# Sparse attention and an ELU feed-forward layer on one core: both halves of a pair's scores issued as one group

## The chip, the cores and the metric

The kernel runs on 1 core of one Trainium2 chip. The metric is the device time of one execution in microseconds, here the median of several runs.

## The reference

Attention over 8 batches, 8 heads, 576 positions, 64 features per head, and behind it a feed-forward layer on the 4608 tokens:

```python
scores = scale * np.matmul(q, k.transpose(0, 1, 3, 2))
mask_local = (rel >= 0) & (rel < stride)                     # heads 0 to 3, stride 32
mask_strided = (rel >= 0) & (pos[None, :] % stride == pos[:, None] % stride)   # heads 4 to 7
...
attn = np.exp(scores)
attn = attn / (np.sum(attn, axis=-1, keepdims=True) + 1e-09)
...
h = x @ w_in                                                 # 512 to 2048
g = np.where(h > 0.0, h, alpha * (np.exp(np.minimum(h, 0.0)) - 1.0))
return (g @ w_out).astype(np.float32)                        # 2048 to 512
```

## The kernel before

**The work.** Each batch has four "pairs" of heads (class `Pair`): s0 and s1 (strided heads), l0 and l1 (local heads). A pair's scores are computed in two halves, u = 0 and 1, as small blocks: a local half has 6 blocks of 128 keys by 96 queries, a strided one 4 blocks of 126 by 126 (u = 0) or 6 of 108 by 108 (u = 1). A score matmul contracts over the 64 features of one head, so it uses 64 rows of TensorE's array; the blocks alternate between the array's upper and lower 64 rows, and the two row halves write to two different PSUM banks (`bank` in `blocks`, L385). `scores(u)` (L413) is: the matmuls into the double bank `pair_a` (L422), one exp on ScalarE from both banks at once (L430), and the multiplication by the mask on VectorE (L437). `av(u)` (L442) multiplies the probabilities by v, whose extra column of ones gives the sum (L454, full array), into a bank of the ring; VectorE takes the reciprocal (L462) and writes the normalised x (L463). `x_out` (L478) transposes x into `xT`. For strided pairs it does five transposes on TensorE (L490) into a ring bank and two ScalarE copies (L497, L499); the first two transposes read what av(0) left, the other three what av(1) left. For local pairs of batches 0 to 3 there are six transposes (L503) and a copy (L507, on VectorE from batch 2 on), the fourth to the sixth for av(1); from batch 4 on a DMA transpose on SP's queue does it (L482).

`transposes` (`t_q`, `t_k`) brings q and k into the layout that scores need, on TensorE with a ring bank and a ScalarE copy. DMA transposes do it instead from batch 3 on for strided pairs (`BY_DMA = 3`) and from batch 4 on for local ones (`EARLY = 4`).

**The feed-forward layer.** Tokens go in nine chunks of 512. `moe_in(nb, m)` (L545) does four 128x512 matmuls into a bank of the ring `hps` (L534), exp on ScalarE (L556) and two VectorE operations that make ELU of it (L563, L565). `moe_out(nb, i)` (L569) does four matmuls into a bank of `ops` (L575); four such calls fill one output block, which ScalarE copies to o_sb (L579) and SP stores (L581).

**The order of the work.** It is written out by hand. Stage nb of the last loop interleaves, for s = 0 to 15, moe_in(nb, s) and moe_out(nb - 1, s), with the attention of batch nb + 1 in between: before each moe_in is an even gap (2s), before each moe_out an odd one (2s + 1). `attention(b, start, pitch, at)` puts pair i's pieces at gap start + pitch * i + offset, with the offsets `at` in the order t_q, t_k, scores(0), scores(1), av(0), av(1), x_out, v_in. From batch 3 on start is 2 and pitch 7, so the four pairs' scores(0) come at gaps 2, 9, 16 and 23. Batch 3 has its strided pairs first, batches 4 to 7 have the local ones first. Each engine works through its own instructions in this order. `halo` (a VectorE copy inside v_loc) stands at av(1)'s offset less 2, for batches before the fifth.

**PSUM.** There are eight banks of 512 floats a partition: `pair_a` (two), `half0` and `half1`, and `single0` to `single3`. `share` says which of them each use takes: `sc` (scores), `hps`, `ops`, `ring` (av, transposes, x_out). A `Ring` gives the bank that was handed out longest ago; whoever is to write it waits for the readers of its last content. Up to batch 3 (stages 1 and 2) hps is half0 and half1, and the ring is single0 to single2. From batch 4 on hps is half0, half1 and single0, and the ring single1 and single2. ops is single3.

The functions that the change touches, and what calls them:

Of the kernel before, what the change touches and what calls it, by code (L numbers as in the profile page):

```python
# [10 lines left out]
F32 = mybir.dt.float32  # L11
# [3 lines left out]
ACT = mybir.ActivationFunctionType  # L15
# [15 lines left out]


PIECES = (-2, -1, 0, 2, 3, 5, 7, 0)
TIMES = (
    None,
    (4, 6, (-3, -2, 0, 2, 4, 6, 9, 3)),
    (6, 6, (-3, -2, 0, 2, 4, 6, 8, 0)),
    (2, 7, PIECES),
)


# [15 lines left out]
def kernel(  # L57
# [9 lines left out]
    nc = tc.nc  # L67
# [4 lines left out]
    scale = 1.0 / float(D) ** 0.5  # L72
# [16 lines left out]
    pair_a = ps.tile([128, 2, 512], F32, tag="pair_a")  # L89
    singles = [ps.tile([128, 512], F32, tag=f"single{i}", name=f"single{i}")  # L90
               for i in range(4)]

    used = []

    class Ring:
# [3 lines left out]
        def next(self):  # L99

            for bank in self.banks:
                if all(bank is not u for u in used):
                    break
            else:
                bank = next(u for u in used if any(u is b for b in self.banks))
                used[:] = [u for u in used if u is not bank]
            used.append(bank)
            return bank


    rings = {}

    def share(sc, hps, ops, ring):
        rings.update(sc=Ring(*sc), hps=Ring(*hps), ops=Ring(*ops), ring=Ring(*ring))
# [41 lines left out]
    EARLY = 4  # L156

    BY_DMA = 3
# [46 lines left out]
    def transpose_batch(b):  # L205

        if b >= BY_DMA:
            for name, to in (("q", qT), ("k", kT)):
                nc.sync.dma_start_transpose(out=to["str"][b % 2],
                                            in_=nat[name, "str"][b % 3])  # L210
        if b >= EARLY:
            for name, to, o in (("q", qT, 0), ("k", kT, 32)):
                for a in range(2):
                    nc.sync.dma_start_transpose(
                        out=to["loc"][b % 2][:, a, o:o + 640].rearrange(
                            "p (i r) -> p i r", r=128),
                        in_=nat[name, "loc"][b % 3][:, 640 * a:640 * a + 640])

    def load_batch(b):
        for name in "qkv":  # L220
            load_strided(b, name)
        for name in "qkv":
            load_local(b, name)
# [97 lines left out]
    class Pair:  # L321
# [89 lines left out]
                nc.vector.tensor_copy(t[0:32, :, 1:6, 0:D], t[96:128, :, 0:5, 0:D])  # L411

        def scores(self, u):  # L413
            sc = rings["sc"].next()
            blocks = self.blocks(u)
            for p, blk, bank, i, nk, nq in blocks:
                at, half = self.place(p, blk)
                d = slice(64 * half, 64 * half + 64)
                kind = "str" if self.strided else "loc"
                c = 0 if self.strided else LB * blk  # L420

                nc.tensor.matmul(sc[:, bank, i * nq:(i + 1) * nq],  # L422
                                 lhsT=kT[kind][self.b % 2][d, at, c:c + 128],
                                 rhs=qT[kind][self.b % 2][d, at, c:c + nq],
                                 start=True, stop=True)
            nk, nq = blocks[0][4:]
            w = len(blocks) // 2 * nq
            pr = (p_p if self.b else p_p0).tile([128, 648], BF16, tag="pr", name="pr")
            halves = pr[0:nk, 0:2 * w].rearrange("k (a x) -> k a x", a=2)
            nc.scalar.activation(halves, sc[0:nk, :, 0:w], ACT.Exp, scale=scale)  # L430
            if not self.strided:
                m = mask_l[:, 288 * u:288 * (u + 1)]
            elif u == 0:
                m = mask_s[0:126, 0:252]
            else:
                m = mask_s3[0:108, 0:324]
            nc.vector.tensor_tensor(halves, halves,  # L437
                                    m.unsqueeze(1).to_broadcast([nk, 2, w]),
                                    op=ALU.mult)
            self.pr[u] = pr  # L440
# [68 lines left out]
    def attention(b, start, pitch, at):  # L509


        gaps = {}
        pairs = [Pair(b, s, hp) for s in (b < EARLY, b >= EARLY) for hp in range(2)]
        if b >= EARLY:
            gaps[start] = [pairs[3].halo]
        for i, pr in enumerate(pairs):
            for off, piece in ((at[0], pr.t_q), (at[1], pr.t_k),
                               (at[7], lambda pr=pr: pr.v_in(0)),
                               (at[7] + (b > 1), lambda pr=pr: pr.v_in(1)),
                               (at[2], lambda pr=pr: pr.scores(0)),  # L520
                               (at[3], lambda pr=pr: pr.scores(1)),
                               (at[4], lambda pr=pr: pr.av(0)),
                               (at[5], lambda pr=pr: pr.av(1)),
                               (at[6] + (b > 1 and pr.strided), pr.x_out), (at[5] - 2, pr.halo if b < EARLY else lambda: None)):
                gaps.setdefault(start + pitch * i + off, []).append(piece)
        return gaps

# [10 lines left out]
    def moe_ahead(c, start, stop):  # L538

        for m in range(AHEAD):  # L540
            if start:
                ahead[m] = rings["hps"].next()
            moe_chunk(0, m, c, ahead[m], start, stop)
# [25 lines left out]
    def moe_out(nb, i):  # L569
        kk, part = divmod(i, 4)  # L570
        if part == 0:
            state["ops"] = rings["ops"].next()
        ops = state["ops"]
        for m in range(4 * part, 4 * part + 4):
            nc.tensor.matmul(ops, lhsT=g_of[nb][:, m, kk * 128:(kk + 1) * 128],  # L575
                             rhs=w_out_sb[:, m, :], start=(m == 0), stop=(m == MC - 1))
        if part == 3:
            o_sb = p_o.tile([128, d_model], F32, tag="o_sb", name="o_sb")
            nc.scalar.copy(o_sb, ops)  # L579
            r0 = nb * N_TILE + kk * 128  # L580
            nc.sync.dma_start(out=out[r0:r0 + 128, :], in_=o_sb)  # L581
# [19 lines left out]
    def range_flag(row_ok16):  # L601
        cnt = rings["ring"].next()
        nc.tensor.matmul(cnt[0:1, 0:1], lhsT=row_ok16, rhs=ones, start=True, stop=True)
        nc.vector.tensor_scalar(flag, cnt[0:1, 0:1], scalar1=127.5, scalar2=None,
                                op0=ALU.is_le)

    def run(gaps, keys):
        for gap in sorted(g for g in gaps if g in keys):
            for piece in gaps[gap]:
                piece()  # L610

    every = range(-10, 1000)
    pairs = {p.name: p for p in (Pair(0, s, hp) for s in (True, False) for hp in range(2))}
    parts = [s for s in OPENING if s.startswith("moe")]
    for step in OPENING:
        pair, what = step.split(".")
        if pair == "moe":
            if step == parts[0]:

                ps_open.close()  # L620
                ps_h = inner.enter_context(tc.tile_pool(name="ps_h", bufs=1, space=PSUM))
                b_halves = [ps_h.tile([128, 512], F32, tag=f"half{i}", name=f"half{i}")
                            for i in range(2)]
                rings["hps"] = Ring(*b_halves, singles[3])
            moe_ahead(int(what), step == parts[0], step == parts[-1])
        else:
            pairs[pair].step(what)
# [13 lines left out]
    for nb in range(n_chunks + 1):  # L641

        if nb + 1 < B:
            gaps = attention(nb + 1, *TIMES[min(nb + 1, 3)])
            if nb == 0:
                share([pair_a], b_halves + singles[3:], [], singles[:3])
            elif nb + 1 < EARLY:
                share([pair_a], b_halves, singles[3:], singles[:3])
            else:
                share([pair_a], b_halves + singles[:1], singles[3:], singles[1:3])  # L650
        else:
            gaps = {}
            share([], b_halves + singles[:1], singles[2:], singles[1:2])
        if nb + 3 < B:
            load_batch(nb + 3)
        for s in range(MC):
            if s == 6 and nb > 0 and nb + 2 < B:
                transpose_batch(nb + 2)
            run(gaps, (2 * s,) if s else range(-10, 1))
            if nb < n_chunks:  # L660
                moe_in(nb, s)
            run(gaps, (2 * s + 1,))
            if nb == B and s == 4:
                range_flag(row_ok16)
            if nb > 0:
                moe_out(nb - 1, s)
        run(gaps, range(2 * MC, 1000))
        if nb + 1 == B:
            row_ok16 = range_check()
# [163 lines left out]
```

## Time and profile before

| what | value |
|---|---|
| median of 3 runs | 335.62 us (335.5 to 335.96) |
| the profiled execution | 335.16 us |
| its span, first to last instruction | 333.4 us |
| TensorE matmuls | 309.0 us busy, 93% of the span |
| VectorE | 246.6 us, 74% |
| ScalarE | 177.0 us, 53% |
| chain that ended last, share of TensorE | 86% |
| mean granted TensorE clock | 0.988 |

PE is TensorE's matmuls, PEld its weight loads, DVE is VectorE, ACT is ScalarE, POOL is GpSimd, SP is the queue of output stores and DMA transposes. In a timeline each row has the start in us from the span's start, the duration, engine, line, operation, what is written and read, the shapes, and how many such instructions were merged into the row (x4). Matmuls are pipelined: the end of one is modelled and lies behind the start of the next, so on TensorE distances of starts are to be read. Some matmul records are missing from the trace (x3 where four were issued). Idle time before an instruction stands in brackets with who ended it.

### The profile page before, as it was taken

How to read it: one execution, taken by the hardware profiler on the slowest of the kernel's cores; microseconds unless marked ns; L12 is line 12 of the kernel's file. 1: busy time of each engine (PE TensorE's matmuls, PEld its weight loads, DVE VectorE, ACT ScalarE, POOL GpSimd, SP SyncE). 2: the span in 40 equal slices, each digit the busy share in tenths (PEclk: the TensorE clock that was granted, in tenths of full speed). 3: DMA queues.
4: the chain of work that ended last, by engine and by line, in shares of the span. 5: the costliest groups of instructions: out<-in, count | busy, mean ns of one | idle time of the engine just before them, and what ended most of it. 6: DMA issues, size and time to landing. Idle time of an engine off the chain costs nothing.

```text
span 333.4 us, 6112 instructions
## 1 busy us (share of the span) xinstructions
PE 309.0 (93%) x2198; PEld 151.8 (46%) x2238; DVE 246.6 (74%) x536; ACT 177.0 (53%) x316; POOL 146.6 (44%) x233
## 2 busy tenths in 40 slices
PE   1887888999999999999999999999999999999993
PEld 0563554455544454444444444444444444444441
DVE  6684699797778778898788878887887666766500
ACT  3744788676555664555655554556555434444220
POOL 8976774998389679919943850000000000000000
PEclk9999699999999999999999999999999999999999
DMA  6999999999989999999998995900110010000111
GB/s 103 144 132 164 161 205 128 122 136 145 161 118 136 148 177 110 112 136 170 169 142 120 166 93 114 142 33 34 49 49 33 31 66 31 31 34 33 64 64 70
DMA packets 102523, 35.68 MB, mean 107 GB/s; under 512 B 80269, under 2 KB 97877, under 8 KB 102485
## 3 DMA queue, kind: packets, MB, share of 16 engines
q0 software_dynamic: 68016, 18.10, 56.6%
q1 hardware_dynamic: 34469, 17.11, 25.7%
q8 instruction: 19, 0.31, 0.4%
q14 instruction: 19, 0.16, 0.2%
HBM read 36.70 MB, written 9.44 MB: 138 GB/s over the span
## 4 chain that ended last, share of the span: by engine, by line
PE 86%; ACT 4%; DVE 4%; issue 2%; DMA 2%; SPq 1%; DVEq 0%; ACTq 0%
PE single L575 37%; PE half L534 28%; PE single L534 9%; PE pair_a L422 4%; PE single L454 4%; DMA q_stage<-in_q_dram 2%; PE single L366 1%; ACT pr L430 1%; PE single L490 1%; SPq L173 1%; PE single L352 1%; ACT e_sb L556 1%; PE single L503 1%; DVE x_l L463 1%; DVE g_sb L565 1%
## 5 line engine op out<-in xcount | busy, mean ns | idle before, releaser
L575 PE MATMUL single<-w_out_sb,g_sb 128*128 128x512 bf16 x561 | 143.4, 379 | 1.1 <-issue 0.5
L534 PE MATMUL half<-xT,w_in_sb 128*128 128x512 bf16 x410 | 110.9, 387 | 2.1 <-issue 1.0
L556 ACT ACTIVATE e_sb<-half 128x512 f32<-128x512 f32 x107 | 63.9, 597 | 79.3 <-PE half L534 74.0
L563 DVE TENSOR_SCALAR e_sb<-e_sb 128x512 bf16<-128x512 f32 x139 | 62.3, 448 | 48.5 <-ACT e_sb L556 46.0
L575 PEld LDWEIGHTS <-g_sb 128*128 128x128 bf16 x576 | 52.9, 98 | 58.9 <-issue 1.1
L534 PEld LDWEIGHTS <-w_in_sb 128*128 128x128 bf16 x576 | 51.9, 100 | 55.4 <-issue 3.7
L565 DVE TENSOR_TENSOR g_sb<-e_sb,half 128x512 bf16<-128x512 bf16 x102 | 70.2, 688 | 3.8
L430 ACT ACTIVATE pr<-pair_a 128x576 bf16<-128x576 f32 (+2 forms) x60 | 39.0, 650 | 12.1 <-PE pair_a L422 11.9
L534 PE MATMUL single<-xT,w_in_sb 128*128 128x512 bf16 x141 | 38.6, 386 | 0.6 <-issue 0.2
L556 ACT ACTIVATE e_sb<-single 128x512 f32<-128x512 f32 x37 | 22.1, 598 | 26.6 <-PE single L534 23.5
L579 ACT COPY o_sb<-single 128x512 f32<-128x512 f32 x36 | 21.1, 587 | 19.1 <-PE single L575 18.4
L173 POOL DMA_DIRECT2D v_raw<-in_v_dram x32 | 20.8, 701 | 19.8 <-DVE v_str L405 17.8
L454 PEld LDWEIGHTS <-pr 128*128 128x128 bf16 (+3 forms) x352 | 21.8, 111 | 16.1 <-issue 3.3
L565 DVE TENSOR_TENSOR g_sb<-e_sb,single 128x512 bf16<-128x512 bf16 x37 | 25.5, 688 | 1.4
L185 POOL DMA_DIRECT2D v_loc<-in_v_dram x32 | 24.5, 816 | 1.4 <-PE pair_a L422 0.7
L173 POOL DMA_DIRECT2D k_str<-in_k_dram x32 | 20.0, 644 | 5.3 <-DMA w_out_sb<-in_moe_w_out_dram 2.9
L173 POOL DMA_DIRECT2D q_str<-in_q_dram x28 | 17.3, 631 | 7.5 <-DMA k_loc<-in_k_dram 4.5
L463 DVE TENSOR_TENSOR x_l<-single,rden 96x384 bf16<-96x384 f32 x32 | 17.7, 554 | 1.1
L463 DVE TENSOR_TENSOR x_s<-single,rden 126x256 bf16<-126x256 f32 (+1 forms) x32 | 15.7, 491 | 1.1
L437 DVE TENSOR_TENSOR pr<-pr,mask_l 128x576 bf16<-128x576 bf16 x32 | 14.4, 453 | 2.3 <-ACT pr L430 2.0
L437 DVE TENSOR_TENSOR pr<-pr,mask_s 126x504 bf16<-126x504 bf16 (+1 forms) x32 | 14.5, 455 | 1.2 <-ACT pr L430 1.2
L197 POOL DMA_DIRECT2D k_loc<-in_k_dram x16 | 12.4, 786 | 1.8 <-PE half L534 0.8
(96 smaller groups left out, 244.6 us busy)
## 6 DMA issues: line engine op xcount, KB each, us to landing
out_dram<-o_sb SPq DMA_DIRECT2D x36, 256.0 KB, 2.5
v_loc<-in_v_dram POOLq DMA_DIRECT2D x32, 72.0 KB, 5.0
k_str<-in_k_dram POOLq DMA_DIRECT2D x32, 67.5 KB, 4.1
v_raw<-in_v_dram POOLq DMA_DIRECT2D x32, 67.5 KB, 4.4
w_in_sb<-in_moe_w_in_dram POOLq DMA_DIRECT2D x4, 512.0 KB, 8.1
w_out_sb<-in_moe_w_out_dram POOLq DMA_DIRECT2D x4, 512.0 KB, 12.6
q_str<-in_q_dram POOLq DMA_DIRECT2D x28, 67.5 KB, 5.5
q_loc<-in_q_dram POOLq DMA_DIRECT2D x4, 288.0 KB, 6.9
```

The lines of the kernel that those rows point to most:

```text
L173: engine.dma_start(out=t[0:108, h].rearrange("p g d -> p (g d)"), in_=rows[h, :, 0:30, :].rearrange("t (r g) d -> t r (g d)", g=5))
L185: nc.gpsimd.dma_start(out=v_loc[b % 3][32:128, h, :, :D], in_=v[b, h].rearrange("(i p) d -> p i d", p=LB))
L430: nc.scalar.activation(halves, sc[0:nk, :, 0:w], ACT.Exp, scale=scale)
L437: nc.vector.tensor_tensor(halves, halves, m.unsqueeze(1).to_broadcast([nk, 2, w]), op=ALU.mult)
L454: nc.tensor.matmul(av[0:m, p, blk - b0, :], lhsT=self.pr[u][0:nk, o:o + m], rhs=vt[0:nk, 2 * self.hp + p, blk, :], start=True, stop=True)
L463: nc.vector.tensor_tensor(self.x[0:nq, b0:b0 + n].rearrange("q g p d -> q p g d"), av[0:nq, :, 0:n, 0:D], r.unsqueeze(3).to_broadcast([nq, ...
L534: nc.tensor.matmul(hps, lhsT=w_in_sb[:, c, m * 128:(m + 1) * 128], rhs=xT[:, c, nb * N_TILE:(nb + 1) * N_TILE], start=start, stop=stop)
L556: nc.scalar.activation(e_sb, hps, ACT.Exp)
L563: nc.vector.tensor_scalar(e1_sb, e_sb, scalar1=1.0, scalar2=1.0, op0=ALU.min, op1=ALU.subtract)
L565: nc.vector.tensor_tensor(g_of[nb][:, m, :], e1_sb, hps, op=ALU.max)
L575: nc.tensor.matmul(ops, lhsT=g_of[nb][:, m, kk * 128:(kk + 1) * 128], rhs=w_out_sb[:, m, :], start=(m == 0), stop=(m == MC - 1))
L579: nc.scalar.copy(o_sb, ops)
```

## The change

From batch 3 on (`b >= BY_DMA`) scores(1) no longer goes to `pair_a`, but to half0 and half1, one row half of the array into each, and stands in the same gap as scores(0), right behind it. Its exp becomes two activations, one for each bank. So the matmuls of both halves follow one another, 12 for a local pair and 10 for a strided one.

The offsets change with it: scores(0) and scores(1) at 0 (before: 0 and 2), av(0) at 3 (as before), av(1) at 4 (5), x_out at 6 (7 for local pairs and 8 for strided ones; the extra gap of strided pairs stays for batch 2 alone). halo, tied to av(1), comes a gap earlier in batch 3.

The banks change places: half0 and half1 become the ring (in stage 2 with single0, later alone), and hps takes single1 and single2 (stage 2) or single0 to single2 (later). How many banks each use has stays as it was. scores(1) takes both halves whenever it runs, and they count as handed out last.

```diff
+WHOLE = (-2, -1, 0, 0, 3, 4, 6, 0)
 TIMES = (
...
-    (2, 7, PIECES),
+    (2, 7, WHOLE),
 )
...
         def scores(self, u):
-            sc = rings["sc"].next()
+            if self.b >= BY_DMA and u == 1:
+                halves = b_halves
+                used[:] = [x for x in used if all(x is not h for h in halves)] + halves
+                sc = [halves[0][:, None, :], halves[1][:, None, :]]
+                sc = [(h, slice(i, i + 1)) for i, h in enumerate(sc)]
+            else:
+                sc = [(rings["sc"].next(), slice(0, 2))]
...
-                nc.tensor.matmul(sc[:, bank, i * nq:(i + 1) * nq],
+                tile_, of = next((t, a) for t, a in sc if a.start <= bank < a.stop)
+                nc.tensor.matmul(tile_[:, bank - of.start, i * nq:(i + 1) * nq],
...
-            nc.scalar.activation(halves, sc[0:nk, :, 0:w], ACT.Exp, scale=scale)
+            for t, of in sc:
+                nc.scalar.activation(halves[:, of], t[0:nk, :, 0:w], ACT.Exp, scale=scale)
...
-                               (at[6] + (b > 1 and pr.strided), pr.x_out), (at[5] - 2, pr.halo if b < EARLY else lambda: None)):
+                               (at[6] + (b == 2 and pr.strided), pr.x_out), (at[5] - 2, pr.halo if b < EARLY else lambda: None)):
...
-            elif nb + 1 < EARLY:
+            elif nb + 1 < BY_DMA:
                 share([pair_a], b_halves, singles[3:], singles[:3])
+            elif nb + 1 < EARLY:
+                share([pair_a], singles[1:3], singles[3:], b_halves + singles[:1])
             else:
-                share([pair_a], b_halves + singles[:1], singles[3:], singles[1:3])
+                share([pair_a], singles[:3], singles[3:], b_halves)
         else:
             gaps = {}
-            share([], b_halves + singles[:1], singles[2:], singles[1:2])
+            share([], singles[:3], singles[3:] + b_halves[:1], b_halves[1:])
```

## The prediction

> **What bounds the kernel now.** I read the page first, then the timeline of TensorE, then those of VectorE and ScalarE, in a stage that does the matmuls of one token chunk and the attention of a batch from the fourth on. The page's first part:
>
> ```profile
> PE 309.0 (93%) x2198; PEld 151.8 (46%) x2238; DVE 246.6 (74%) x536; ACT 177.0 (53%) x316; POOL 146.6 (44%) x233
> ```
>
> The waits put only 0.5 us of TensorE's idle time between 93 and 300 us to another engine. So there its instruction stream is the time, and what it saves or newly waits for is won or lost whole. Its timeline (start, duration, line):
>
> ```profile
> 179.26 0.32 PE L422 MATMUL pair_a<-qT_str,kT_str 64*128 64x108 bf16 x6
> 179.51 1.04 PE L534 MATMUL half<-xT,w_in_sb 128*128 128x512 bf16 x4
> 180.38 0.32 PE L454 MATMUL single<-v_str,pr 126*128 126x65 bf16 x4
> 180.54 1.03 PE L575 MATMUL single<-w_out_sb,g_sb 128*128 128x512 bf16 x4
> 181.40 1.03 PE L534 MATMUL half<-xT,w_in_sb 128*128 128x512 bf16 x4
> 182.26 0.37 PE L454 MATMUL single<-v_str,pr 108*128 108x65 bf16 x6
> 182.47 1.03 PE L575 MATMUL single<-w_out_sb,g_sb 128*128 128x512 bf16 x4
> 183.34 1.03 PE L534 MATMUL single<-xT,w_in_sb 128*128 128x512 bf16 x4
> 184.30 0.28 PE L422 MATMUL pair_a<-qT_str,kT_str 64*128 64x126 bf16 x4
> ```
>
> Read the distances of starts, not the durations, which overlap. Four big matmuls last 0.86 us until the next group (180.54 to 181.40), but 0.96 when a score group follows (183.34 to 184.30), and 0.87 right after one (179.51 to 180.38). So a score group costs 0.10 us to enter and 0.01 behind it. Then VectorE and ScalarE:
>
> ```profile
> 182.31 0.17 DVE L462 RECIPROCAL rden<-single 126x4 f32<-126x4 f32 x1
> 182.52 0.42 DVE L463 TENSOR_TENSOR x_s<-single,rden 126x256 bf16<-126x256 f32 x1
> 183.10 0.43 DVE L563 TENSOR_SCALAR e_sb<-e_sb 128x512 bf16<-128x512 f32 x1 [0.15 <-ACT e_sb L556]
> 183.56 0.69 DVE L565 TENSOR_TENSOR g_sb<-e_sb,half 128x512 bf16<-128x512 bf16 x1
> 184.16 0.19 DVE L462 RECIPROCAL rden<-single 108x6 f32<-108x6 f32 x1
> 184.39 0.56 DVE L463 TENSOR_TENSOR x_s<-single,rden 108x384 bf16<-108x384 f32 x1
> ```
>
> ```profile
> 184.40 0.60 ACT L556 ACTIVATE e_sb<-single 128x512 f32<-128x512 f32 x1 [1.34 <-PE single L534]
> 184.90 0.58 ACT L430 ACTIVATE pr<-pair_a 126x504 bf16<-126x504 f32 x1
> 185.59 0.59 ACT L579 COPY o_sb<-single 128x512 f32<-128x512 f32 x1
> ```
>
> VectorE works in order and is late: av(0) starts at 180.38, its reciprocal at 182.31, since the ELU of the moe_in ahead of it (L563, L565) comes first. av(1) starts at 182.26 and its x is written at 184.39 + 0.56 = 184.95, 2.69 us later. ScalarE starts an independent operation 0.09 us before the one ahead ends, and an e_sb 0.21 us after its four matmuls are through (those of 183.34 are at 184.20; e_sb starts at 184.40).
>
> **What the merge saves.** It touches batches 3 to 7: 5 x 4 = 20 pairs, each with two score groups now and one then. In the order of the built program 10 (strided) or 12 (local) score matmuls stand in one stretch. Per pair one entry (0.10) and one 0.01 go. The exit shrinks too: the six matmuls at 179.26 last 0.32, of which the last takes 0.216 (mean of that form), so they start within 0.10, two steps of 0.05 for pairs that run side by side; the next group starts 0.25 after the first, so leaving takes 0.14-0.15. Merged, one such exit becomes a step of 0.05: 0.09 saved. Together 0.20, for local pairs the same (0.235 long, last start at 0.10). 20 x 0.20 = **4.0 us saved**. No group of such length on two tiles is in the trace. Bounds: only the entry goes (20 x 0.11 = 2.2), or the exit costs nothing more (20 x 0.255 = 5.1). I take 4.0, as the steps inside a group are measured.
>
> The Trainium skill (TensorEngine Tiling (Array Packing), Tiling Modes, Key Properties) says that a change of the tiling mode drains TensorE, and the extra 0.10 and 0.09 us agree. Its page TensorE: Matmul & The Clock Gate (Step-by-step: what each phase is for) has about 128 cycles for a drain, 53 ns at 2.4 GHz; an estimate from it is 20 x 2 x 0.053 = 2.1 us saved, and the sum below would be 1.9 us slower.
>
> **What the new order makes TensorE wait for.** A gap is a group of four big matmuls, 0.86 us. Strided x_out was 3 gaps after av(1); now it is 2 (3, 4, 6 against 3, 5, 8). So the transposes that read av(1)'s x (the third on) are due 0.21 + 2 x 0.86 + 0.12 = 2.05 us after av(1) starts. In-order TensorE holds everything behind them.
>
> - *Second strided pair (s1).* Scores fall on an odd gap, so av(1) stands right behind a moe_in, as at 182.26 above. x is there after 2.69 plus 0.06 for the signal, that is 0.70 late. Batches 4 to 7: 2.8. In batch 3 a t_q lies between (0.38 + 0.10), but halo's copy (0.60) is moved a gap ahead in VectorE's queue; I take 0.47 (bounds 0.22 and 0.70).
> - *First strided pair (s0).* av(1) now precedes the next moe_in's ELU. av(0)'s x is written 182.94 - 180.38 = 2.56 after av(0) starts; av(1)'s reciprocal and multiply follow (0.19 + 0.03 + 0.56 less 0.09): 3.24, and av(1) starts 0.16 + 0.86 after av(0). So 2.22 + 0.06 - 2.05 = 0.23 late, five times: 1.15.
> - *Last local pair of batch 3.* The same move from an even to an odd gap: 0.69 late where 0.11 is paid already; 0.58 more. That one shows that TensorE does pay: its six transposes last 0.54 instead of 0.42.
>
> ```profile
> 92.92 0.42 PE L503 MATMUL single<-identity,x_l 96*128 96x96 bf16 x6
> ```
> ```profile
> 126.65 0.54 PE L503 MATMUL single<-identity,x_l 96*128 96x96 bf16 x6
> ```
>
> VectorE wrote that x at 126.28 + 0.55 = 126.83.
>
> - *o_sb behind three exps.* s1's merged group stands just ahead of moe_out(11), which ends an output block. There is one output bank (single3), so moe_out(12) waits for the copy L579. One exp of 108x648 (0.709) becomes two of 108x324. Not in the trace; the rows 504, 576 and 648 wide (0.591, 0.650, 0.709) give 0.178 + 0.82 ns each, so 0.445 (bounds 0.355, half the row, and 0.591, the next narrower row). From the group's start at 0: e_sb 0.11-0.71, exp 0.62-1.21, 1.12-1.57, 1.48-1.92, o_sb 1.83-2.42, seen at 2.48; TensorE asks after 0.37 + 0.87 + 0.86 = 2.10. So 0.37 late, five times: 1.85 (bounds 0.95 and 3.3).
> - *Batch 3, first local pair.* t_k now queues its ScalarE copy behind x_out's two: 0.1 late.
>
> Sum: 2.8 + 0.47 + 1.15 + 0.58 + 1.85 + 0.1 = **6.95 us of waits**. The x_s terms are bounded by the 0.11 that is paid today at that distance (10 x 0.11 = 1.1 of the 4.4) and by 0.70 everywhere (7.0).
>
> **At no cost.** The exps add about 0.18 of ScalarE time per pair, but it has 45% idle, and av(0) follows three gaps later as before; without that cover each gap lost would be 0.86. Bank counts of hps, ring and ops stay the same (batch 3: two, three, one; later three, two, one); only which banks they are changes. s1's scores now wait for x_out's copies of s0 in half0: the copies end 1.0 us after the transposes, the matmul comes after 0.86 + 0.10 + 0.12 = 1.08. That margin is thin: 0.1 x 5 if it fails. On SP's queue an x_l transpose moves ahead of an output store; it is due half a stage later. POOL's loads keep their order, and k and q for the merged group landed a stage before.
>
> **The sum.** The profiled execution took 335.16 us (span 333.4 and 1.76 around it). 335.16 - 4.0 + 6.95 = 338.1. The median shown (335.62) is 0.46 above that execution, so I forecast **338.5**, about 0.9% slower. This case's own range is 337.2 to 340.
>
> **Rivals.**
> - *Waits are covered (faster).* If VectorE wrote each x within 2.05 us of av(1), and o_sb came in time, only the saving is left: 335.6 - 4.0 = 331.6. For it: no wait is seen today. Against: 2.69 on VectorE is measured, and the 0.54 above. Chance 0.10.
> - *Half of it.* Only the odd-gap waits are real (2.8 + 0.47 + 0.58 = 3.85), s0 and o_sb are covered: 335.6 - 4.0 + 3.85 = 335.5. Chance 0.12, mostly within 0.2%.
> - *Exps decide (slower still).* With 0.591 per half the o_sb wait is 0.66: 338.5 + 5 x 0.29 = 340.0; much the same if only the entry is saved (338.5 + 1.8 = 340.3). Chance 0.13. The Trainium skill (TensorEngine Tiling (Array Packing), PSUM Bottleneck) warns that tiling speeds TensorE and not the emptying of PSUM; the o_sb term is that, by these rows.
> - *The change doesn't do what it says:* the groups stay split. The built order excludes it nearly; 0.02, at 338.5 + 4.0 = 342.5.
>
> My forecast has 0.63. **Chances:** faster by over 0.2% 0.13, within 0.2% (about what a measurement can tell) 0.09, slower 0.78. The range 335.4 to 340.4 leaves out the faster rival and little above.
>
> **What would show it.** Score groups of 10 and 12 in one stretch about 0.36 us long, one 0.96 instead of two per pair. TensorE's x transposes (x_out) of the two strided pairs held 0.2 and 0.7 us by VectorE's x; the first matmul of moe_out(12) held 0.4 by o_sb. The forecast is wrong if those transposes start unheld, or if the steps inside a merged group grow at the change of banks.

## The result, and the profile after

The changed kernel takes 337.17 us (median of 20 runs, 335.5 to 339.93), the kernel before 334.54 (20 runs, 332.28 to 335.96): the ratio is 1.0085, with a 95% interval of 1.006 to 1.0109. It is slower by 2.8 us by that ratio, by 2.6 between the medians. The forecast was 338.5 against 335.62, a ratio of 1.0086.

The runs of one kernel spread over about 4 us, and the traces differ by up to 2.8 us in the opening, before the change begins to act (told at the end). So traces are compared stage by stage: the time from the last o_sb copy of one stage to that of the next.

| stage does attention of batch | 3 | 4 | 5 | 6 | 7 | none (the 8th) | none (the 9th) | sum |
|---|---|---|---|---|---|---|---|---|
| before, us | 35.83 | 32.39 | 32.39 | 32.39 | 32.39 | 27.63 | 27.83 | 220.84 |
| after, us | 37.17 | 32.90 | 32.87 | 32.84 | 32.84 | 27.63 | 27.83 | 224.08 |

All of the difference between these sums, 3.24 us, lies in the five stages where scores are merged. (The spans of the two traces differ by 3.9: another 0.2 lies ahead of these stages and 0.4 behind them.) The page's first part, after:

```profile
PE 307.2 (91%) x2199; PEld 153.1 (45%) x2238; DVE 244.9 (73%) x536; ACT 176.6 (52%) x336; POOL 147.8 (44%) x233
```

TensorE has less to do and takes longer: it is now idle in the middle. The waits of TensorE between 93 and 300 us (us in total, times, longest), where before there was only the 0.5 for xT:

```profile
PE half L499 <- DVE x_s L472: 2.4, 5, 0.6
PE single L584 <- ACT o_sb L588: 0.9, 5, 0.2
...
PE half L512 <- DVE x_l L472: 0.7, 1, 0.7
PE single L543 <- DVE xT L516: 0.5, 1, 0.5
PE single L499 <- DVE x_s L472: 0.4, 1, 0.4
```

(L499 and L512 are the transposes of x_out, L472 the multiply that writes x, L584 moe_out, L588 the o_sb copy.) These sums are too small, since a matmul's modelled end lies about 0.17 us behind the time at which the next could start; distances of starts show the whole. TensorE's timeline for the second strided pair of batch 5:

```profile
186.27 0.28 PE L430 MATMUL pair_a<-qT_str,kT_str 64*128 64x126 bf16 x4
186.39 0.31 PE L430 MATMUL half<-qT_str,kT_str 64*128 64x108 bf16 x6
186.63 1.04 PE L584 MATMUL single<-w_out_sb,g_sb 128*128 128x512 bf16 x4
187.51 1.03 PE L543 MATMUL single<-xT,w_in_sb 128*128 128x512 bf16 x4
188.71 1.02 PE L584 MATMUL single<-w_out_sb,g_sb 128*128 128x512 bf16 x4 [0.17 <-ACT o_sb L588]
189.57 0.32 PE L463 MATMUL half<-v_str,pr 126*128 126x65 bf16 x4
189.72 1.03 PE L543 MATMUL single<-xT,w_in_sb 128*128 128x512 bf16 x4
190.58 0.37 PE L463 MATMUL half<-v_str,pr 108*128 108x65 bf16 x6
...
191.66 1.03 PE L543 MATMUL single<-xT,w_in_sb 128*128 128x512 bf16 x4
192.52 0.28 PE L499 MATMUL half<-identity,x_s 126*128 126x126 bf16 x2
193.35 0.32 PE L499 MATMUL half<-identity,x_s 108*128 108x108 bf16 x3 [0.55 <-DVE x_s L472]
```

The merged group is 0.36 us long (186.27 to 186.63): the step from the first half to the second takes 0.12 for four matmuls, and nothing is lost at the change of banks. Then two holes. Four big matmuls take 1.20 us instead of 0.86 (187.51 to 188.71): 0.34 until o_sb is copied. Two transposes take 0.83 instead of 0.12 (192.52 to 193.35): 0.71 until av(1)'s x is there. VectorE ahead of it:

```profile
191.41 0.46 DVE L572 TENSOR_SCALAR e_sb<-e_sb 128x512 bf16<-128x512 f32 x1 [0.39 <-ACT e_sb L565]
191.90 0.69 DVE L574 TENSOR_TENSOR g_sb<-e_sb,single 128x512 bf16<-128x512 bf16 x1
192.51 0.19 DVE L471 RECIPROCAL rden<-half 108x6 f32<-108x6 f32 x1
192.73 0.56 DVE L472 TENSOR_TENSOR x_s<-half,rden 108x384 bf16<-108x384 f32 x1
```

av(1) starts at 190.58, its x is written at 193.29: 2.71 us, as the 2.69 of before. VectorE even waits for e_sb (0.39): what holds av(1)'s reciprocal is the chain moe_in, exp, ELU of the same gap, which stands ahead of it in the order. ScalarE shows the other hole:

```profile
186.44 0.60 ACT L565 ACTIVATE e_sb<-single 128x512 f32<-128x512 f32 x1 [0.22 <-PE single L543]
186.93 0.58 ACT L439 ACTIVATE pr<-pair_a 126x504 bf16<-126x504 f32 x1
187.40 0.78 ACT L439 ACTIVATE pr<-half 108x324 bf16<-108x324 f32 x2
188.04 0.61 ACT L588 COPY o_sb<-single 128x512 f32<-128x512 f32 x1
```

moe_out(11) was through at 187.51, but its copy stood behind the pair's three exps and ended at 188.65; moe_out(12), due at 188.37, began at 188.71. The waits of the first strided pair and of batch 3's last local pair:

```profile
184.78 0.70 PE L499 MATMUL half<-identity,x_s 126*128 126x126 bf16 x5
```
```profile
126.55 0.29 PE L512 MATMUL half<-identity,x_l 96*128 96x96 bf16 x3
127.59 0.30 PE L512 MATMUL half<-identity,x_l 96*128 96x96 bf16 x3 [0.74 <-DVE x_l L472]
```

Five strided transposes take 0.42 without a wait and 0.70 here. Three local ones take 0.13 until the next and 1.04 here.

### The profile page after: what moved, and what is told of

Same layout as the page of the kernel before. It is cut to its first block, busy times and chain, and to the rows that moved or that the text cites. A ratio compares the mean times of both kernels' runs of the same rounds, so it can differ in the third digit from the quotient of the medians.

```text
span 337.3 us, 6160 instructions
## 1 busy us (share of the span) xinstructions
PE 307.2 (91%) x2199; PEld 153.1 (45%) x2238; DVE 244.9 (73%) x536; ACT 176.6 (52%) x336; POOL 147.8 (44%) x233
## 4 chain that ended last, share of the span: by engine, by line
PE 43%; POOL 19%; DMA 18%; issue 7%; DVE 4%; ACT 4%; SPq 2%; ACTq 0%; POOLq 0%
PE single L543 19%; PE single L584 16%; PE half L584 6%; DMA v_loc<-in_v_dram 5%; DMA w_in_sb<-in_moe_w_in_dram 4%; DMA k_str<-in_k_dram 4%; DMA w_out_sb<-in_moe_w_out_dram 4%; POOL v_raw L174 3%; POOL k_str L174 3%; POOL v_loc L186 2%; ACT pr L439 2%; DVE x_s L472 2%; ACT e_sb L565 2%; DVE g_sb L574 1%; POOL k_loc L198 1%
## 5 line engine op out<-in xcount | busy, mean ns | idle before, releaser
L543 PE MATMUL single<-xT,w_in_sb 128*128 128x512 bf16 x455 | 120.3, 382 | 1.6 <-issue 0.5
L584 PE MATMUL single<-w_out_sb,g_sb 128*128 128x512 bf16 x465 | 119.4, 379 | 2.2 <-issue 0.9
L565 ACT ACTIVATE e_sb<-single 128x512 f32<-128x512 f32 x117 | 70.1, 599 | 95.2 <-PE single L543 91.7
L574 DVE TENSOR_TENSOR g_sb<-e_sb,single 128x512 bf16<-128x512 bf16 x117 | 80.5, 688 | 4.4
L584 PEld LDWEIGHTS <-g_sb 128*128 128x128 bf16 x576 | 53.6, 98 | 61.8 <-issue 3.4
L543 PE MATMUL half<-xT,w_in_sb 128*128 128x512 bf16 x100 | 30.1, 414 | 0.9 <-issue 0.5
L439 ACT ACTIVATE pr<-pair_a 128x576 bf16<-128x576 f32 (+2 forms) x40 | 25.4, 636 | 7.5 <-PE pair_a L430 7.4
L565 ACT ACTIVATE e_sb<-half 128x512 f32<-128x512 f32 x27 | 16.1, 598 | 15.3 <-PE half L543 15.3
L584 PE MATMUL half<-w_out_sb,g_sb 128*128 128x512 bf16 x93 | 23.5, 379 | 0.2
L588 ACT COPY o_sb<-single 128x512 f32<-128x512 f32 x30 | 17.7, 592 | 11.3 <-PE single L584 10.4
L574 DVE TENSOR_TENSOR g_sb<-e_sb,half 128x512 bf16<-128x512 bf16 x22 | 15.1, 688 | 0.8
L439 ACT ACTIVATE pr<-half 108x324 bf16<-108x324 f32 (+1 forms) x40 | 14.9, 433 | 0.0
```

What stands on the lines that cost most here:

```text
L439: nc.scalar.activation(halves[:, of], t[0:nk, :, 0:w], ACT.Exp, scale=scale)
L543: nc.tensor.matmul(hps, lhsT=w_in_sb[:, c, m * 128:(m + 1) * 128], rhs=xT[:, c, nb * N_TILE:(nb + 1) * N_TILE], start=start, stop=stop)
L565: nc.scalar.activation(e_sb, hps, ACT.Exp)
L574: nc.vector.tensor_tensor(g_of[nb][:, m, :], e1_sb, hps, op=ALU.max)
```

## The experiments

The theory: TensorE gains what the merge promises, and loses more by x_out, which comes two gaps after av(1) instead of three, and by o_sb, which stands behind the exps. The rival: the time goes to the split exps (twenty more ScalarE instructions) and to half0 and half1 as the ring, whatever x_out's place.

| kernel | median, us | ratio to before (95%) | stages 3 to 7, us | their sum with the two behind, less before |
|---|---|---|---|---|
| before | 333.88 (25 runs beside e1 to e4) | | 35.83, 32.39, 32.39, 32.39, 32.39 | |
| after | 337.17 (20 runs, beside 20 of before at 334.54) | 1.0085 (1.006 to 1.0109) | 37.17, 32.90, 32.87, 32.84, 32.84 | +3.24 |
| e1, x_out late | 333.15 | 0.9977 (0.9945 to 1.0009) | 36.27, 31.86, 31.87, 31.86, 31.86 | -1.67 |
| e2, x_out early, no merge | 338.88 | 1.0107 (1.0056 to 1.0158) | 36.83, 33.08, 33.08, 33.08, 33.08 | +3.76 |
| e3, x_out at 9 and 8 | 331.55 | 0.9925 (0.989 to 0.9961) | 35.29, 31.55, 31.56, 31.55, 31.55 | -3.90 |
| e4, two ops banks | 335.76 | 1.0066 (1.0031 to 1.0101) | 36.73, 32.88, 32.85, 32.51, 32.51 | +2.10 |
| e5, e4 without late loads | 342.31 (one run, beside one of before at 335.62) | | 36.79, 32.51, 32.52, 32.51, 32.51 | +1.47 |

**e1: the changed kernel, strided x_out late again.**

```diff
-(at[6] + (b == 2 and pr.strided), pr.x_out)
+(at[6] + (b == 2 and pr.strided) + 2 * (b > 2 and pr.strided), pr.x_out)
```

> The changed kernel with strided x_out put back from offset 6 to 8 in batches 3 to 7 (merged scores, split exps, banks and av(1) as changed). Theory (x_out comes too early after av(1)): the VectorE waits of the strided transposes go (0.27 + 0.71 us per batch in the trace after), and x_out then stands between moe_out(11) and moe_out(12), so the o_sb wait (0.34) goes too from batch 4 on; in return s0's x_out must wait for the exp that reads half0 of s1's scores, about 0.4 per batch. About 1.4 us below the kernel before (4.2 saved, some 2.7 of waits left, batch 3's local one among them). Rival (the time is lost to the split exps and to half0 and half1 as the ring): no gain over the changed kernel, 2.8 us above the kernel before.

Measured: 1.67 below the kernel before by stages, 4.9 below the changed one, and by medians not to be told from before. The VectorE waits of the strided transposes are gone, and the o_sb wait is left once, in batch 3 (0.2 by the waits, 0.34 by distances of starts). The last local pair of batch 3 waits 1.06 us here. The expected new wait is there, on the exp of half0; by distances of starts it is 0.34 in each of batches 4 to 7, where 0.4 was expected:

```profile
183.26 0.41 PE L499 MATMUL half<-identity,x_s 126*128 126x126 bf16 x5 [0.17 <-ACT pr L439]
```

The exps are split here as in the changed kernel and the ring is the same, so the rival falls as the account of the loss. These 0.34 us are what the split exp and the new ring cost at this place of x_out.

**e2: the kernel before, with x_out's new distance alone.**

```diff
-(at[6] + (b > 1 and pr.strided), pr.x_out)
+(at[6] + (b == 2 and pr.strided), pr.x_out)
```

> The kernel before with one edit: strided x_out a gap earlier in batches 3 to 7 (offset 7, two gaps after av(1), as in the changed kernel). No merge, no split exp, old banks. Theory: s0's av(1) follows a moe_in directly (odd gap), so its x is 0.70 us late each time; s1's av(1) is on an even gap and the wait is nil to 0.1. 4 x 0.70 + 0.7 in batch 3 = 2.8 to 3.5 us slower than the kernel before. Rival (x_out's place matters little): within 0.5 us of the kernel before.

Measured: 3.76 us longer in the stages, 0.69 in each of batches 4 to 7. The timeline, batch 5:

```profile
186.33 0.28 PE L490 MATMUL single<-identity,x_s 126*128 126x126 bf16 x2
187.13 0.32 PE L490 MATMUL single<-identity,x_s 108*128 108x108 bf16 x3 [0.52 <-DVE x_s L463]
...
194.37 0.42 PE L490 MATMUL single<-identity,x_s 126*128 126x126 bf16 x5
```

The pair whose av(1) stands behind a moe_in pays 0.69 (0.80 for two transposes); the one whose av(1) stands ahead of a moe_in pays nothing (0.42). The sum lies above the expected 2.8 to 3.5, as batch 3's stage is 1.00 longer: VectorE's TENSOR_SCALAR ahead of the late x took 0.71 there and not 0.43. One gap of distance, without any merge, costs more by stages than the whole change does.

**e3: the changed kernel, with x_out where nothing is late.**

```diff
-(at[6] + (b == 2 and pr.strided), pr.x_out)
+(at[6] + (b == 2 and pr.strided) + (b > 2 and (3 - pr.hp if pr.strided else pr.hp)), pr.x_out)
```

> The changed kernel with x_out of s0 at offset 9, of s1 at 8 (batches 3 to 7) and of batch 3's second local pair at 7. Theory: all x waits go, and s0's x_out no longer stands next to the exp of half0; what is left is o_sb (0.1 per batch from batch 4 on, 0.35 in batch 3). 4.2 saved less 0.8: about 3.4 us below the kernel before, 6 below the changed one. If the merge saved only the entry (2.3 us), 1.5 below the kernel before. Rival (split exps and ring cost the time): at or above the kernel before.

(The edit also puts the second local pair's x_out, a DMA transpose, a gap later in batches 4 to 7.)

Measured: 3.90 us shorter in the stages and 0.75% by medians: it beats both kernels. Each of the last four stages is 0.84 shorter than before. Both transposes run unheld, and so does the rest:

```profile
180.08 0.28 PE L430 MATMUL pair_a<-qT_str,kT_str 64*128 64x126 bf16 x4
180.20 0.30 PE L430 MATMUL half<-qT_str,kT_str 64*128 64x108 bf16 x6
180.44 1.04 PE L584 MATMUL single<-w_out_sb,g_sb 128*128 128x512 bf16 x4
181.31 1.03 PE L543 MATMUL single<-xT,w_in_sb 128*128 128x512 bf16 x3
182.18 0.42 PE L499 MATMUL half<-identity,x_s 126*128 126x126 bf16 x5
182.45 1.02 PE L584 MATMUL single<-w_out_sb,g_sb 128*128 128x512 bf16 x4
...
187.99 0.42 PE L499 MATMUL half<-identity,x_s 126*128 126x126 bf16 x5
```

With no wait of TensorE left in the last four stages, 0.84 / 4 = 0.21 us is what merging one pair saves; twenty pairs make 4.2. The split exps, still there, cost nothing in these stages. s0's x_out now also stands between moe_out(11) and moe_out(12), and the 0.1 that was still expected of o_sb does not show. In batch 3 o_sb's wait stays (0.34).

**e4: two banks for ops.**

```diff
-                share([pair_a], singles[:3], singles[3:], b_halves)
+                share([pair_a], singles[:2], singles[2:], b_halves)
...
-            share([], singles[:3], singles[3:] + b_halves[:1], b_halves[1:])
+            share([], singles[:2] + b_halves[:1], singles[2:], b_halves[1:])
```

> The changed kernel with the banks shared out otherwise from batch 4 on: two for ops, two for hps (before: one and three). Theory: moe_out(12) no longer waits for the o_sb copy that stands behind three exps, 0.34 us in each of 4 stages: 1.4 us below the changed kernel, some 1.5 above the kernel before; x waits stay. If two banks for hps are too few, TensorE waits for VectorE at moe_in after scores, and the gain is eaten. Rival (the o_sb wait is no loss, as work behind it catches up): same as the changed kernel.

Measured: the o_sb wait is gone from batch 4 on, but only two of the four stages gain it (32.51 against 32.84, 0.33); those of batches 4 and 5 stay at 32.88 and 32.85. Two banks for hps were enough: no wait of moe_in for VectorE shows. In the stages of batches 4 and 5 the x wait of s1 grew from 0.75 and 0.72 to 1.05 and 1.02 us. Of the 1.14 us by which e4 is shorter than after in sum, 0.44 lies in batch 3's stage, where the two programs are the same (see e5). VectorE in batch 4, and below in batch 6, at the same place:

```profile
155.16 0.80 DVE L572 TENSOR_SCALAR e_sb<-e_sb 128x512 bf16<-128x512 f32 x1
155.99 0.69 DVE L574 TENSOR_TENSOR g_sb<-e_sb,single 128x512 bf16<-128x512 bf16 x1
156.59 0.19 DVE L471 RECIPROCAL rden<-half 108x6 f32<-108x6 f32 x1
```
```profile
220.89 0.43 DVE L572 TENSOR_SCALAR e_sb<-e_sb 128x512 bf16<-128x512 f32 x1
221.35 0.69 DVE L574 TENSOR_TENSOR g_sb<-e_sb,single 128x512 bf16<-128x512 bf16 x1
221.95 0.19 DVE L471 RECIPROCAL rden<-half 108x6 f32<-108x6 f32 x1
```

TENSOR_SCALAR takes 0.80 instead of 0.43, and that is the growth of the wait. GpSimd was issuing loads at that time:

```profile
154.04 3.14 POOL L198 DMA_DIRECT2D k_loc<-in_k_dram  x4
```

**e5: e4 without the loads of batches 5 to 7.**

```diff
-        if nb + 3 < B:
+        if nb + 3 < 5:
             load_batch(nb + 3)
+        elif nb + 3 < B:
+            raw[nb + 3] = raw[nb + 1]
...
-            engine.memset(t[96:128, :, 8 * D:], 0.0)
+            engine.memset(t[96:128], 0.0)
```

> The kernel with two ops banks from batch 4 on (e4), with the loads of batches 5, 6 and 7 left out (their attention works on what older batches left in the buffers), and the fill of the local q and k buffers made wider for it, in the opening. In e4 the stages that do batches 4 and 5 took 32.88 and 32.85 us from o_sb to o_sb, those of batches 6 and 7 took 32.51; in the first two GpSimd was issuing loads, and VectorE's TENSOR_SCALAR of the ELU took up to 0.80 us instead of 0.43. Theory (GpSimd's load issues lengthen VectorE's chain ahead of av(1)'s x): without them TENSOR_SCALAR takes 0.43 in all stages, s1's x wait falls from 1.05 to 0.73 us, the stages of batches 4 and 5 take 32.5 like the other two, and batch 3's takes 36.2 to 36.4 instead of 36.7 (s0 0.23 instead of 0.37, l1 0.7 instead of 0.9 as in the trace after). Rival (the bank order in those stages makes the difference): 32.9 as in e4.

Measured: 32.51 and 32.52 in the stages of batches 4 and 5, as in the other two; TENSOR_SCALAR takes 0.41 to 0.43 in all four, and s1 waits 0.69. The rival of the bank order falls.

Batch 3's stage is 36.79, not 36.2 to 36.4. The expectation took its waits from the trace of after. In e4 itself, with the loads being issued, s0 waited 0.28 there, s1 0.51 and l1 0.67, and in e5 they wait as long, so there was nothing to gain. After and e4 are the same program up to there, and the longer wait of l1 in after (0.91) is that of one row of VectorE ahead of its x; after, then e4:

```profile
125.46 0.66 DVE L572 TENSOR_SCALAR e_sb<-e_sb 128x512 bf16<-128x512 f32 x1 [0.36 <-ACT e_sb L565]
```
```profile
122.67 0.43 DVE L572 TENSOR_SCALAR e_sb<-e_sb 128x512 bf16<-128x512 f32 x1 [0.36 <-ACT e_sb L565]
```

GpSimd was issuing loads beside both. So load issues can lengthen the chain that holds av(1)'s x, by 0.2 to 0.4 us where one delays a row of it, and from one execution to the next it is not the same row.

The run as a whole is longer than all others, by its opening, where the fill was made wider. VectorE's copy into v_str takes 7.41 us there, and 0.28 to 0.29 at its other six places in this trace; six of GpSimd's fills run beside it, and TensorE then waits 4.3 us for VectorE. The copy, and the first of the fills:

```profile
62.09 7.41 DVE L406 COPY v_str<-v_raw 126x512 bf16<-126x512 bf16 x1
```
```profile
62.47 1.35 POOL L240 MEMSET q_loc<- 32x1280 bf16 x1
```

## Why the prediction was right, and where its terms were off

- **The number.** 337.17 lies just below the range of 337.2 to 340 that the prediction gave for its own case, because before itself came out at 334.54 over 20 runs and not at the 335.62 of three. Against its own before, the change cost what was forecast. Two small misses offset each other in part: the saving and the waits were both forecast too small, by 0.2 and 0.5 us.
- **The merge: 4.0 forecast, 4.2 measured** (e3: 0.84 a stage for four pairs). The steps inside a group are 0.04 to 0.06 for a pair that runs side by side, and neither the second tile nor the two single banks add to them. Bounds of 2.2 and 5.1 were not needed. The estimate from the Trainium skill (TensorE: Matmul & The Clock Gate, Step-by-step: what each phase is for; 2.1 us for two drains of 53 ns) was half of it: a change of mode cost 0.10 in and 0.11 out, and the measurement decides.
- **s1's x: 0.70 forecast, 0.68 to 0.75 measured** in batches 4 to 7 (mean 0.71). The distance from av(1) to its x could be read in before, at another pair with the same neighbour.
- **s0's x: 0.23 forecast, 0.27 to 0.28 measured** in batches 4 to 7. With o_sb's wait there as well, the rival that only the odd-gap waits are real falls.
- **o_sb: 0.37 forecast, 0.34 measured.** An exp 324 wide takes 0.448 (forecast 0.445 by a line through three rows), one of 288 takes 0.418.
- **Batch 3 was sized too small:** 1.75 forecast, 2.17 measured (s0 0.36, s1 0.61, t_k 0.06, o_sb 0.34, l1 0.91 less the 0.11 of before). The terms took undisturbed VectorE rows; in that stage GpSimd issues loads nearly all the time. Where no load issue delays the row ahead of its x (e4, e5), l1 waits 0.67, and 0.69 was forecast. The 0.11 of before goes with such a delay too: its TENSOR_SCALAR at 124.69 took 0.73.
- **The sum:** 6.95 of waits forecast and 7.45 measured (4 x 1.32 + 2.17); with the 4.2 this gives 3.25 against 3.24 by stages. The whole forecast was +2.9, the ratio gives 2.8 (2.0 to 3.6 by the interval).
- **The margins that were costed at nothing held:** the wait of s1's scores for x_out's copies in half0 shows in no timeline of after, and no wait of after is put down to hps, ring or POOL's order.
- **The rival of exps as the bound** (after the Trainium skill, TensorEngine Tiling (Array Packing), PSUM Bottleneck) is true in one place, o_sb, and e3 shows that moving x_out hides it there too, from batch 4 on.

## What to carry to other kernels

Where the engine that bounds a kernel works in order, ask of each moved instruction not how long its input takes to compute, but what stands ahead of that input on the other engine; an x_out one gap earlier, while its x still stood behind an ELU in VectorE's order, cost 0.7 us a batch here. A merge that saves switches (0.21 us each) is worth doing only with the distances that feed it kept: the same merge gives +0.85% or -0.75% by the place of the x_out transposes alone. Look for a second place of the same kind in the trace of before, since it holds the latency that the change will meet.

## What the runs showed of the hardware

**VectorE's TENSOR_SCALAR against GpSimd's load issues.** From f32 to bf16, 128x512, it ran 544 times in the seven traces behind 93 us with no GpSimd instruction beside it, and never took over 0.43 us, though in 188 of these the DMA engines were more than half busy. So the transfers alone do not delay it. Of the 245 that ran beside a GpSimd instruction over half took 0.43 as well and the others up to 0.80; all 66 of over 0.5 ran beside a DMA issue. TENSOR_TENSOR into g_sb stayed at 0.69 throughout. The mean over the kernel fell from 0.451 (e4) to 0.433 without the late loads (e5):

```profile
L572 DVE TENSOR_SCALAR e_sb<-e_sb 128x512 bf16<-128x512 f32 x139 | 62.7, 451 | 48.2 <-ACT e_sb L565 46.1
```
```profile
L572 DVE TENSOR_SCALAR e_sb<-e_sb 128x512 bf16<-128x512 f32 x139 | 60.2, 433 | 52.0 <-ACT e_sb L565 50.1
```

The Trainium skill (SBUF — State Buffer, Who interferes with whom) says that tensor_scalar can contend with GpSimd for a port pair that the two engines share, when its operands meet certain conditions, and that tensor_tensor has no such mode but contends with GpSimd's reads when both its inputs are in SBUF. The rows agree (0.80 against an unchanged 0.69, with one input of that TENSOR_TENSOR in PSUM).

**VectorE beside GpSimd's fills.** In six of the seven traces one VectorE instruction near 64 us lasts about until the series of GpSimd's fills beside it is over: the copy into v_str 2.30 us in before, 1.41 in after, 1.19 in e4, a TENSOR_SCALAR 2.23 in e1 and 1.82 in e2. These fills are 256 elements wide and last 0.34 to 0.87 us each; in e5 they are 1280 wide and last 1.35, and the copy takes 7.41. e3 shows no such row.

**The opening's clock.** In some executions TensorE is granted less clock between 30 and 40 us from the start. Of the traces here before, after and e2 have a mean of 0.66 there, e1, e3, e4 and e5 have 1.00 (after, then e3; the clock stands behind POOL's count):

```profile
30.00:40.00 10.00, 7.32 (x48) 3.75 (x47) 6.29 (x14) 7.83 (x14) 5.91 (x9) 0.66 1.45 172
```
```profile
30.00:40.00 10.00, 6.98 (x81) 4.16 (x83) 7.99 (x19) 9.48 (x19) 6.49 (x9) 1.00 1.53 176
```

In before it is 0.50 from 32.2 to 39.0 us. The stage of batch 3 begins at 93.1 to 93.6 us in the first three and at 90.8 to 91.3 in e1, e3 and e4, nearly as much apart as the whole effect studied. The runs of after sort by it: the seven with a mean granted clock below 0.99 took 338.5 to 339.9 us, the others 335.5 to 337.4; those of e4 do not sort as well. That the clock makes all of this difference is not shown. The Trainium skill (TensorE: Matmul & The Clock Gate, Part 1) has the clock at half after an idle window of about 3.4 us. The drop in e5 (0.50 from 69.3 to 76.2) agrees, as no matmul ran in the 3.4 us ahead of it; but in before matmuls were busy for 1.63 us of the 3.42 ahead of the drop, so what sets it off there stays open.
